# Attention and MLP on one core: another order of the same instructions on each engine

## The chip, the cores and the metric

The kernel runs on one core of a Trainium2 chip. The metric is device time in microseconds for one call, on the device's own clock. The engines of the core run side by side, each through its own queue in order: TensorE (matmuls; PE in the profile, its weight loads PEld), VectorE (DVE), ScalarE (ACT), and SyncE (SP), which here issues every transfer. An instruction that waits holds back all that stands behind it on its engine.

## The reference

Rotary attention over 4 batches, 8 heads, 576 positions, head size 64, and an MLP on its output (2304 rows, 512 to 2048 to 512).

```python
q_rot, k_rot = (rotate(q), rotate(k))
scores = scale * np.matmul(q_rot, k_rot.transpose(0, 1, 3, 2))
attn = np.exp(scores - np.max(scores, axis=-1, keepdims=True))
attn = attn / (np.sum(attn, axis=-1, keepdims=True) + 1e-09)
attn_out = np.matmul(attn, v)
# heads side by side: x is (2304, 512)
h = x @ w_in
g = np.where(h >= 1, h, np.where(h <= -1, 0.0, (h + 1) ** 2 / 4.0))
out = g @ w_out
```

## The kernel before

Every product is made of three half-precision matmuls: each float32 operand is split into a high part and the rest, in float16, and high·high, high·low and low·high are summed in PSUM. So K, Q, V, the attention weights, the attention output, the MLP's inner values and both weight matrices all pass through ACT (high part) and DVE (rest).

The work runs in eight blocks: for each batch a first one (row tiles 0 and 1 of 128 rows) and a last one (tiles 2 and 3, with the 64 rows left over). In a block, for each of four head pairs and each tile: `scores` (line 597; 12 matmuls into the two banks of `psS`; line 614 for the left rows), then the softmax on DVE and ACT (lines 570 to 582): negative maximum on DVE (L570), exponential with row sum on ACT (L572), reciprocal on DVE (L577), high part on ACT (L580) and rest on DVE (L582) into `phl`. A DMA transpose on SP (`dmaT`, L246) turns `phl` into `pT`. When the tiles of a head pair are there, 28 matmuls make the values (`values`, L632, into `psV`), and `x_out` (L643 ACT, L646 DVE) splits them into `xT`. The MLP of a block (`mlp_block`) runs after its attention: eight steps `m` of 2 × 12 matmuls (L711, into `psH`), an activation on ACT and DVE (L719 to L734) and 2 × 6 matmuls into `psO` (L743); at the end ACT brings `psO` out (L754) and SP stores it.

Beside the first blocks the weights are prepared: `prep_w` loads each of eight slices of `w_in` and `w_out` in two pieces (`dma`, L242), into buffers that are in use for something else before and after (other slices, `rv`, `kT`). DVE unpacks them (L518 to L522), ACT takes the high part (L531), and the rest comes from DVE (L540) or from TensorE and ACT (L549 to L553). `prep_v` splits V (ACT L462 high, DVE L466 rest; `vS`) and copies parts of it within SBUF (`vM`, three transfers). `prep_k` and `load_q` load K and Q of the next batch.

The order is written out by hand. Each piece of work enters a list with `plan.add` (engine, cost, what it reads and writes): 2,224 steps, 487 on TensorE, 751 on ACT, 777 on DVE, 209 on SP. `Plan.order` walks through the string `ORDER`: each number takes that element out of the steps still left. The steps are then emitted in that order, so each engine gets its own steps in it, and the waits follow from the data. The costs given to `plan.add`, with the transfer rates in `dma` (L242) and `dmaT` (L246), are not read when the kernel is built. Buffers are assigned when the steps are listed, not when they are emitted. A "place" below is a step's position in the order of its engine, counted from 0.

Of the kernel before, what the change touches and what calls it, by code (L numbers as in the profile page):

```python
# [24 lines left out]

ORDER = """
# [58 lines left out]
"""  # L85

PICK = set("""  # L90
lo0 lo12 lo15 m1.2 m1.6 m2.0 m2.1 m2.2 m2.3 m2.4 m2.7 m3.0 m3.1 m3.2 m3.3 m3.4 m3.5 m4.0 m4.1 m4.3 m5.2 m5.3
m5.4 m5.5 m6.0 m6.1 m6.2 m6.4 m6.5 m6.6 m6.7 m7.2 m7.4 m7.5 m8.2 m8.4 m8.5 m9.0 m9.1 m9.2 m9.3 v0 v1
""".split())
O_CHUNKS = 5


class Plan:
# [41 lines left out]
    def order(self, idle):  # L139
        left = list(range(len(self.steps)))  # L140
        return [partial(idle, *map(int, k[1:].split("."))) if k[0] == "*" else self.steps[left.pop(int(k))][3]
                for k in ORDER.split()]
# [3 lines left out]
def kernel(  # L146
# [12 lines left out]
    nc = tc.nc  # L159
    B, _, NP, S = km.shape[1:]  # L160
# [22 lines left out]
    vS = sbt("vS", [128, 2, T, H, D], F16)  # L183
# [734 lines left out]
```

## Time and profile before

| | us |
|---|---|
| median of 3 runs (613.07 to 615.18) | 614.44 |
| the profiled execution | 611.8 |
| its span, first to last instruction | 610.0 |
| PE / PEld busy | 569.6 / 367.9 |
| DVE / ACT busy | 483.2 / 457.7 |
| mean granted TensorE clock | 0.982 |

The first 100 us prepare operands while little of the attention runs; up to some 215 us attention, weights and the first MLP run together; from then on TensorE has a queue of MLP work. How to read the views: a row of the timeline names the start, the duration, the engine, the line, the operation, the tiles and their shapes; brackets at its end give how long the engine sat idle ahead of it and what ended the idle time. "PEclk" is the granted clock as a share of full speed (1.00 is 2.4 GHz, 0.50 is 1.2 GHz).

### The profile page before, as it was taken

What the parts mean: (1) busy time and instruction counts of PE and PEld (TensorE: products, weight loads), DVE (VectorE), ACT (ScalarE), POOL (GpSimd) and SP (SyncE); (2) the same over time, 40 slices, a digit from 0 to 9 for tenths busy, and PEclk for the clock granted to TensorE, in tenths of its full rate; (3) what the DMA queues carried; (4) which work ended last, traced back from release to release, by engine and by line L of the source; (5) the groups of instructions that cost most, each with busy time, mean ns of one, the idle gap of its engine ahead of it and who ended that gap; (6) DMA issues with size and microseconds to landing.
All of it is one profiled execution on the core that took longest, in us unless ns stands there. A gap on an engine that the chain in (4) does not pass through costs nothing.

```text
span 610.0 us, 12165 instructions
## 1 busy us (share of the span) xinstructions
PE 569.6 (93%) x4824; PEld 367.9 (60%) x4824; DVE 483.2 (79%) x782; ACT 457.7 (75%) x922; POOL 1.5 (0%) x11
## 2 busy tenths in 40 slices
PE   5677779999999969999999999999999999999996
PEld 3352435556666646666666766666666676667673
DVE  5998898999999959999889888987978757524341
ACT  4999787999999848788866788868876677553431
POOL 1000000000000000000000000000000000000000
PEclk9889898999999989999999999999999999999999
DMA  8889996685959978857599577575563836500000
GB/s 281 302 198 289 264 254 155 187 209 104 221 168 199 237 120 169 172 104 111 156 187 181 92 164 162 119 129 85 103 128 64 130 66 131 99 36 1 1 36 18
DMA packets 184009, 88.94 MB, mean 146 GB/s; under 512 B 170768, under 2 KB 172048, under 8 KB 183952
## 3 DMA queue, kind: packets, MB, share of 16 engines
q1 hardware_dynamic: 183952, 88.17, 65.5%
q8 instruction: 38, 0.62, 0.4%
q14 instruction: 19, 0.16, 0.1%
HBM read 38.60 MB, written 4.72 MB: 71 GB/s over the span
## 4 chain that ended last, share of the span: by engine, by line
PE 60%; DVE 8%; ACT 4%; DMA 3%; issue 1%; SPq 1%; ACTq 0%
PE psO L743 24%; PE psH L711 24%; PE psV L632 6%; PE psS L597 5%; DVE phl L582 2%; DMA pT<-phl 2%; DVE sca L570 2%; ACT p L572 1%; SPq L246 1%; DMA rv<-in_vm_dram 1%; DVE r L730 1%; PE psS L614 1%; ACT phl L580 1%; DVE g L734 1%; DMA vM<-vS 1%
## 5 line engine op out<-in xcount | busy, mean ns | idle before, releaser
L711 PE MATMUL psH<-xT,w 128*128 128x256 f16 (+1 forms) x1920 | 205.7, 262 | 0.6 <-ACT a L719 0.6
L743 PE MATMUL psO<-w,g 128*128 128x512 f16 x864 | 201.5, 379 | 0.0
L711 PEld LDWEIGHTS <-w 128*128 128x128 f16 x1920 | 170.7, 98 | 36.8 <-issue 5.0
L743 PEld LDWEIGHTS <-g 128*128 128x128 f16 x864 | 81.8, 98 | 84.6 <-DVE g L734 1.5
L572 ACT ACTIVATE p<-psS,sca 128x576 f32<-128x576 f32 x144 | 105.3, 734 | 26.3 <-DVE sca L570 18.1
L580 ACT ACTIVATE phl<-p,sca 128x576 f16<-128x576 f32 x144 | 108.2, 768 | 22.3 <-DVE sca L577 16.4
L582 DVE SCALAR_TENSOR_TENSOR phl<-p,sca,phl 128x576 f16<-128x576 f32 x144 | 115.9, 811 | 10.2 <-ACT phl L580 10.0
L570 DVE TENSOR_REDUCE sca<-psS 128x1 f32<-128x576 f32 x144 | 105.2, 750 | 14.3 <-PE psS L597 14.1
L734 DVE SCALAR_TENSOR_TENSOR g<-r,g 128x512 f16<-128x512 f32 x72 | 49.4, 686 | 32.5 <-ACT g L732 32.3
L597 PE MATMUL psS<-kT,qT 64*128 64x512 f16 (+1 forms) x768 | 61.3, 288 | 6.6 <-ACT p L572 6.4
L719 ACT ACTIVATE a<-psH 128x512 f32<-128x512 f32 x72 | 42.3, 587 | 33.0 <-PE psH L711 27.0
L730 DVE SCALAR_TENSOR_TENSOR r<-a,r 128x512 f32<-128x512 f32 x72 | 49.4, 687 | 20.1 <-ACT r L728 19.2
L732 ACT ACTIVATE g<-r 128x512 f16<-128x512 f32 x72 | 44.8, 623 | 26.4 <-DVE r L730 16.2
L597 PEld LDWEIGHTS <-qT 64*128 64x128 f16 x768 | 29.9, 95 | 50.0 <-issue 27.9
L632 PE MATMUL psV<-pT,vS 128*64 128x256 f16 (+1 forms) x512 | 44.3, 298 | 6.9 <-DMA pT<-phl 6.9
L632 PEld LDWEIGHTS <-vS 128*64 128x64 f16 x512 | 27.6, 114 | 14.3 <-DMA pT<-phl 7.3
L723 DVE SCALAR_TENSOR_TENSOR r<-a 128x512 f32<-128x512 f32 x38 | 26.1, 687 | 5.8 <-ACT a L719 4.5
L572 ACT ACTIVATION_READ_ACCUMULATOR p<-psS,sca 128x1 f32 x144 | 28.4, 197 | 0.0
L632 PE MATMUL psV<-pT,vM 128*64 128x256 f16 (+1 forms) x320 | 26.8, 300 | 0.1
L643 ACT ACTIVATE xT<-psV,sca 128x320 f16<-128x320 f32 (+1 forms) x24 | 13.7, 569 | 15.3 <-PE psV L632 15.3
L726 ACT ACTIVATE r<-a 128x512 f32<-128x512 f32 x34 | 21.3, 626 | 4.8 <-DVE g L734 4.5
L577 DVE RECIPROCAL sca<-sca 128x2 f32<-128x2 f32 x72 | 11.5, 160 | 15.9 <-ACT sca L575 15.3
(108 smaller groups left out, 486.4 us busy)
## 6 DMA issues: line engine op xcount, KB each, us to landing
w<-in_w_in_dram SPq DMA_DIRECT2D x14, 512.0 KB, 6.4
w<-in_w_out_dram SPq DMA_DIRECT2D x12, 512.0 KB, 7.9
rv<-in_vm_dram SPq DMA_DIRECT2D x8, 512.0 KB, 5.3
out_dram<-o SPq DMA_DIRECT2D x16, 256.0 KB, 2.5
rk<-in_km_dram SPq DMA_DIRECT2D x6, 576.0 KB, 5.7
dup<-in_km_dram SPq DMA_DIRECT2D x6, 576.0 KB, 4.5
rq<-in_qb_dram SPq DMA_DIRECT2D x4, 640.0 KB, 5.2
vM<-vS SPq DMA_DIRECT2D x8, 256.0 KB, 5.1
```

What stands on the lines that cost most here:

```text
L570: plan.add("dve", dve_cost(S, psum=True), at, lambda m=m, src=src: nc.vector.tensor_reduce(out=m, in_=src, op=ALU.max, axis=AX.X, negate=T ...
L572: plan.add("act", act_cost(S, psum=True, ptrs=2), at, lambda a=a, e=e, m=m, src=src: nc.scalar.activation(out=p32[e], in_=src, func=AF.Exp ...
L580: plan.add("act", act_cost(S), at, lambda a=a, e=e, hi=hi: nc.scalar.activation(out=hi, in_=p32[e], func=AF.Copy, scale=rr[:, a:a + 1]), r ...
L582: plan.add("dve", dve_cost(S, ptrs=1), at, lambda a=a, e=e, hi=hi, lo=lo: nc.vector.scalar_tensor_tensor(out=lo, in0=p32[e], scalar=rr[:, ...
L597: nc.tensor.matmul(out=psS[a][:, lo:hi], lhsT=qT[hf][d, l, j, c:c + 128], rhs=kT[ks][d, j, m, lo:hi], start=z == 0, stop=z == 2)
L632: nc.tensor.matmul(out=outs[a], lhsT=st, rhs=moving(a, blk), start=z == 0, stop=z == len(seq) - 1)
L711: nc.tensor.matmul(out=psH[:, n * i:n * i + n], lhsT=wi[ft // 2][:, wl, kk, 128 * (ft % 2):128 * (ft % 2) + 128], rhs=xfn(xl, kk), start=z ...
L719: plan.add("act", act_cost(512, psum=True, ptrs=0), at, lambda one=one: nc.scalar.activation(out=a, in_=psH, func=AF.Relu, scale=2.0 ** -7 ...
L730: plan.add("dve", dve_cost(512), at, lambda one=one: nc.vector.scalar_tensor_tensor(out=r, in0=a, scalar=one, in1=r, op0=ALU.max, op1=ALU. ...
L732: plan.add("act", act_cost(512, ptrs=0), at, lambda g=g, one=one: nc.scalar.activation(out=g[:, 0], in_=r, func=AF.Relu, scale=1.0, bias=- ...
L734: plan.add("dve", dve_cost(512), at, lambda g=g, one=one: nc.vector.scalar_tensor_tensor(out=g[:, 1], in0=r, scalar=-one, in1=g[:, 0], op0 ...
L743: nc.tensor.matmul(out=psO[pos[tt]], lhsT=g[:, gl, n * i + 128 * tt:n * i + 128 * tt + 128], rhs=wo[ft // 2][:, wl, ft % 2, :], start=ft = ...
```

## The change

`ORDER` is replaced by another list of the same length, found by a search over a cost model whose numbers were measured anew. In the plan the rate of an ordinary transfer goes from 400 to 329 bytes per ns, that of the copies within SBUF (`vM`) to 220, that of a transpose from 221 to 231 for 128 rows and to 195 for 64. The unused `idle` (extra matmuls for starred entries of the list) goes. No step is added or removed.

```diff
 ORDER = """
-5 4 1 2 28 1 0 3 51 1 76 27 0 23 47 3 3 25 95 118 95 116 95 46 129 129 157 226 146 71 21 3 0 8 2 20 0 41 16 18 3
+5 4 4 9 1 2 26 4 1 0 0 75 48 51 25 122 121 98 22 46 70 3 25 21 3 129 128 91 91 1 2 4 3 2 2 17 0 16 13 17 55 31
...
-2 3 3 3 3 0 0 0 0 0 0 0 0 0 1 0
+2 3 3 3 8 3 7 7 2 2 2 1 0 0 0 0 0 0 0 0 0 0 1 0
 """
...
-    def order(self, idle):
+    def order(self):
         left = list(range(len(self.steps)))
-        return [partial(idle, *map(int, k[1:].split("."))) if k[0] == "*" else self.steps[left.pop(int(k))][3]
-                for k in ORDER.split()]
+        return [self.steps[left.pop(int(k))][3] for k in ORDER.split()]
...
-    def dma(at, dst, src, r, w, nbytes, eng="sp", chain=[]):
+    def dma(at, dst, src, r, w, nbytes, eng="sp", chain=[], rate=329.0):
...
-        plan.add(eng, 480.0 if eng == "sp" else 1000.0, at, lambda: q.dma_start(out=dst, in_=src), r, w + chain, bw=nbytes / 400.0)
+        plan.add(eng, 480.0 if eng == "sp" else 1000.0, at, lambda: q.dma_start(out=dst, in_=src), r, w + chain, bw=nbytes / rate)
...
-        plan.add("sp", nbytes / 221.0 + 60.0, at,
-                 lambda: nc.sync.dma_start_transpose(out=dst, in_=src), r, w, bw=nbytes / 221.0, turn=True)
+        rate = 231.0 if src.shape[0] == 128 else 195.0
+        plan.add("sp", nbytes / rate + 60.0, at,
+                 lambda: nc.sync.dma_start_transpose(out=dst, in_=src), r, w, bw=nbytes / rate, turn=True)
...
-    def idle(b, n):
-        bank = (psH, psO[0], psO[1], psV, psS[0], psS[1])[b]
-        for _ in range(n):
-            nc.tensor.matmul(out=bank[:, 0:128], lhsT=idn, rhs=idn, start=True, stop=True)
-
-    order = plan.order(idle)
+    order = plan.order()
```

## Rows read from the trace of the kernel before

**Rows 1.** The page, first part: busy us, share, instructions of each engine.

```profile
PE 569.6 (93%) x4824; PEld 367.9 (60%) x4824; DVE 483.2 (79%) x782; ACT 457.7 (75%) x922; POOL 1.5 (0%) x11
```

**Rows 2.** Busy us of each engine by stretch; at the end clock, DMA share, GB/s.

```profile
0.00:58.00 58.00, 38.85 (x173) 23.08 (x173) 49.75 (x116) 47.72 (x107) 1.53 (x11) 0.91 0.88 267
58.00:98.00 40.00, 30.45 (x228) 16.13 (x227) 31.77 (x44) 29.61 (x59) 0.00 (x0) 0.91 1.07 255
98.00:213.00 115.00, 113.04 (x935) 70.95 (x937) 113.34 (x170) 110.20 (x217) 0.00 (x0) 1.00 0.79 182
...
230.00:605.40 375.40, 375.03 (x3364) 249.40 (x3362) 277.70 (x438) 260.37 (x521) 0.00 (x0) 1.00 0.54 107
```

**Rows 3.** The chain of waits in order of time: start, us, what.

```profile
213.98 5.76 DMA pT<-phl
...
502.68 2.73 PE psH L711 x24
505.40 3.88 PE psO L743 x18
```

**Rows 4.** Timeline of TensorE: three matmuls that follow idle time.

```profile
64.89 1.51 PE L549 MATMUL psO<-xT 128*128 128x512 f32 x2 [4.39 <-ACT w L553]
...
92.40 0.71 PE L632 MATMUL psV<-pT,vS 128*64 128x256 f16 x8 [2.08 <-DMA pT<-phl]
...
219.79 1.06 PE L632 MATMUL psV<-pT,vS 128*64 128x256 f16 x8 [4.78 <-DMA pT<-phl]
```

**Rows 5.** Timeline of DVE: three that follow idle time, and one split.

```profile
61.96 0.69 DVE L518 TENSOR_SCALAR o<-w 128x1024 uint32<-128x1024 uint32 x1 [3.71 <-DMA w<-in_w_out_dram]
...
82.52 0.81 DVE L582 SCALAR_TENSOR_TENSOR phl<-p,sca,phl 128x576 f16<-128x576 f32 x1
...
96.00 0.75 DVE L646 SCALAR_TENSOR_TENSOR xT<-psV,sca,xT 128x512 f16<-128x512 f32 x1 [2.56 <-ACT xT L643]
...
223.70 1.42 DVE L570 TENSOR_REDUCE sca<-psS 128x1 f32<-128x576 f32 x2 [6.10 <-PE psS L597]
```

**Rows 6.** Timeline of ACT: the second half of V, and a wait.

```profile
45.99 1.14 ACT L462 ACTIVATE vS<-rv,sca 128x1024 f16<-128x1024 f32 x1
...
63.49 0.78 ACT L580 ACTIVATE phl<-p,sca 128x576 f16<-128x576 f32 x1 [3.25 <-DVE sca L577]
```

**Rows 7.** Timeline of SP's DMA queue, 40 to 100 us.

```profile
41.77 4.31 SPq L246 DMA_TRANSPOSE pT<-phl  x1
...
51.25 1.16 SPq L242 DMA_DIRECT2D w<-in_w_out_dram  x2
...
81.46 8.94 SPq L246 DMA_TRANSPOSE pT<-phl  x2
```

**Rows 8.** Timeline of SP's DMA queue, 198 to 232 us.

```profile
198.74 8.91 SPq L246 DMA_TRANSPOSE pT<-phl  x2
207.70 0.58 SPq L242 DMA_DIRECT2D dup<-in_km_dram  x1
...
208.86 23.12 SPq L246 DMA_TRANSPOSE pT<-phl  x6
```

**Rows 9.** Tile `pT`, its transposes, 36:100 and 230:420: ns min/median/max.

```profile
L246 SPq DMA_TRANSPOSE pT<-phl x8: 3287/4142/9409, 36.0 to 91.6; - x8
...
L246 SPq DMA_TRANSPOSE pT<-phl x40: 1199/2666/5735, 229.5 to 419.3; - x40
```

**Rows 10.** By stretch, as rows 2: two with a lower clock.

```profile
66.00:69.00 3.00, 3.00 (x24) 1.88 (x24) 3.00 (x4) 3.00 (x9) 0.00 (x0) 0.51 1.05 266
...
219.70:223.00 3.30, 3.21 (x32) 2.45 (x34) 0.00 (x0) 0.13 (x1) 0.00 (x0) 0.57 0.77 144
```

**Rows 11.** DMA issues of the page: count, KB each, median us to landing.

```profile
w<-in_w_out_dram SPq DMA_DIRECT2D x12, 512.0 KB, 7.9
...
vM<-vS SPq DMA_DIRECT2D x8, 256.0 KB, 5.1
```

**Rows 12.** By stretch, as rows 2: the first 20 us of the full queue.

```profile
230.00:250.00 20.00, 20.00 (x188) 13.66 (x187) 19.19 (x32) 16.01 (x34) 0.00 (x0) 1.00 0.98 184
```

More of the change, by code (lines that the diff above doesn't have):

```diff
@@ L1 @@
 from contextlib import ExitStack
-from functools import partial
 import numpy as np
@@ L484, in prep_v @@
             r=["rvL", fk, ("vM", 0)], w=["vZ"])
-        dma(at, vM[0:64, 1:5], vS[64:128, 0], [("vS", 0, hf) for hf in range(2)], [("vM", 1)], 64 * 4096)
-        dma(at, vM[64:128, 0:4], vS[0:64, 0], [("vS", 0, hf) for hf in range(2)], [("vM", 2)], 64 * 4096)
-        dma(at, vM[64:128, 4], vM[0:64, 0], [("vM", 0)], [("vM", 3)], 64 * 1024)
+        dma(at, vM[0:64, 1:5], vS[64:128, 0], [("vS", 0, hf) for hf in range(2)], [("vM", 1)], 64 * 4096, rate=220.0)
+        dma(at, vM[64:128, 0:4], vS[0:64, 0], [("vS", 0, hf) for hf in range(2)], [("vM", 2)], 64 * 4096, rate=220.0)
+        dma(at, vM[64:128, 4], vM[0:64, 0], [("vM", 0)], [("vM", 3)], 64 * 1024, rate=220.0)
     vkeys = [("vS", l, hf) for l in range(2) for hf in range(2)] + [("vS", 1, hf, 0) for hf in range(2)] + [("vM", i) for i in range(4)] + ["vZ"]
```

112 rows, old and new, of the table ORDER are left out of this document.

## Prediction

> **What bounds the kernel now.** I read first the page's busy line [rows 1], then busy time by stretch [rows 2], then the chain of waits in order of time [rows 3], and from where the chain leaves TensorE the timelines of each engine [rows 4 to 8]. In [rows 2] see two regimes. From 230 to 605.4 us TensorE is busy 375.03 of 375.40 us, at full clock: nothing but its own queue matters there, and a reorder inside it gains nothing. Before, it idles: 58 − 38.85 = 19.2 us up to 58, 9.6 us from 58 to 98, 2.0 from 98 to 213. From 98 to 213 DVE is as full as TensorE (113.3 and 113.0 of 115). So every us of TensorE idle that goes before 230 comes off the end, provided DVE and ACT lose as much idle there.
>
> The Trainium skill ("Trainium Kernel Development and Optimization", Performance Expectations) says that matmul busy time misleads, since matmuls are pipelined, and that the weight loads' busy share is the better measure. By it TensorE would be 60% used [rows 1], and the reorder could also gain after 230 us, where weight loads fill 249 of 375 us. The trace decides otherwise: twenty-four 256-column matmuls take 2.73 us in the chain and eighteen of 512 take 3.88 us [rows 3], 114 and 216 ns apiece, 107 and 213 ns being the columns at 2.4 GHz. The array is full; I take no gain there.
>
> The idle that can go has three places outside the start:
> - A, 60.5 to 64.9: TensorE waits 4.39 us for ACT [rows 4], which waits 3.25 us for DVE [rows 6], which waits 3.71 us for a w_out load [rows 5]. The load was issued at 51.25 [rows 7] and used at 61.96. Then the clock is down: granted 0.51 from 66 to 69, the 1.2 GHz level, TensorE busy all of it [rows 10]: 3.0 × 0.49 = 1.5 us.
> - B, 90 to 96: TensorE waits 2.08 us for a transpose [rows 4], DVE then 2.56 us [rows 5].
> - C, 215 to 219.8: TensorE waits 4.78 us for a transpose [rows 4], DVE 6.10 us for scores queued behind that on TensorE [rows 5]. The clock again: 0.57 for 3.3 us [rows 10], 3.2 × 0.43 = 1.4 us.
>
> **The change part by part.** No instruction is added or taken away. The rates in the helpers feed only the plan's costs, which nothing reads when the list is followed; the removed `idle` was not used, since the list has no starred entry. Both cost nothing. What is left is the order. I laid both lists against the plan's 2,224 steps: 156 of 487 TensorE steps leave their place (by at most 8), 338 of 751 on ACT, 391 of 777 on DVE, 98 of 209 on SP. For each step I added the work ahead of it on its engine, at the time from its start to the next start in the traced run, in the old and the new order; "ahead +x" is the difference.
>
> A. On SP the two w_out pieces of slice 2 stood at places 32 and 39 and now stand at 33 and 31, ahead of the transpose of head pair 1 (place 30, now 34; issued at 41.77 for 4.31 us [rows 7]). Loads that nobody needs yet move behind: w_out of slice 6 into `rv` from 36 and 48 to 56 and 55, w_in of slice 7 into `kT` from 41 to 61; both pieces of slice 3 and the vM copies pass behind too. The pieces should leave by the 46.1 at which that transpose ended. With the old 10.7 us from issue to use they land at 56.8, with the 7.9 us median of w_out loads [rows 11] at 54. DVE reaches the instruction at 61.96 − 3.71 = 58.25 and has +0.1 us ahead. So DVE's 3.7 us go; TensorE's 4.4 and the clock's 1.5 can go only as far as DVE and ACT follow. Gain between 3.7 and 5.9; I take 4.5, nearer the DVE row, since DVE sets the pace there. What is late next: two vM copies now wait at the head of SP (places 39 and 38) for ACT's second half of V [rows 6], +7.9 us ahead: 47.1 + 7.9 = 55.0. Landing 5.1 us later [rows 11], at 60.1, against TensorE's first values step at 66.8 − 4.4 = 62.4. The cover is 2.3 us; if the copies take the 10.7 us of the load above, it costs 3.3 us.
>
> B. Four transposes now follow each other (places 45 to 48; before 46, 49, 53, 54), with loads of slices 4 to 6 behind. The fourth went out at the end of the pair issued at 81.46 and 8.94 us long [rows 7]. DVE wrote the last of its data by 83.3 [rows 5] and has −1.7 us ahead of that now, so it should go at about 81.6 minus what A brings, and take 3.3 us, the shortest of that stretch [rows 9], and be through by 85. The values step then waits for nothing. Gain: 2.1 (TensorE) to 2.6 (DVE), plus up to another 1.5 of clock; I take 2.5. Behind these transposes now wait the second w_out piece of slice 4 and w_in of slice 5: they leave at about 85 less A's gain, where the old ones left at 80; DVE comes to the first of them at 87 less that gain, with +4.4 us ahead, so 6 us of cover stand against the 7.9 of a median load, and up to 1.9 us are owed if nothing else yields.
>
> C. On TensorE four steps, 4.8 us of work (three of the MLP at 1.3 us [rows 3] and a scores step), move ahead of the last two values steps of the block. On SP the K load at 207.70 and the Q load behind it, which ran before the transposes from 208.86 [rows 8], change place: K's from 102 to 92, Q's from 103 to 110. DVE's 6.10 us go with it, as the scores step now stands before the values. What is late next is the row of transposes itself: the first of it must wait for an earlier values step, which let it go at 198.74 [rows 8] and is also 4.8 us later, so it starts at 203.5. Four of them at 2.67 us (median from 230 to 420 [rows 9]) end at 214.2, at 5 us at 223.5; TensorE wants the last at 219.8, where the old one landed. With most loads gone from between them I take some 3.3 us each, 216.7, no wait. Gain 4.8 to 6.2, taken 5.5; with 5 us each 3.7 less.
>
> The start (0 to 58) is crowded by ACT and DVE (47.7 and 49.8 of 58 busy [rows 2]). At 58 both have the same work ahead (ACT +0.2, DVE +0.1). DVE fills early idle with K and Q products; ACT's first exponentials come 0.7 us sooner in its queue, while the maxima they wait for have +1.7 us ahead on DVE, so ACT idles up to 2.3 us there. From −2 (gain) to +2: I take 0.
>
> The rest (98 to 213, and after 230): TensorE has no idle to lose, so an order can only cost. Of some 325 steps after 230, ten are now ahead of the ACT step they need by more than their old slack, by 1.4 to 2.7 us, in three clusters (253 to 310, 490 to 510, 584); ACT and DVE can run ahead in most of it. Between 0 and 7.1 us (the largest of each cluster: 2.3 + 2.7 + 2.1); I take 2.5.
>
> Sum: 4.5 + 2.5 + 5.5 − 2.5 = 10.0 us. The profiled execution took 611.8 us, of it 610.0 the span; the median of the runs is 614.44, 2.6 us more, spread 2.1. The difference has nothing to do with the order, so I take 10.0 off the median: 604.4.
>
> **The rivals.**
> 1. One of the gains is lost. Either the transposes of C still take 5 us each (C then gives 5.5 − 3.7 = 1.8), or TensorE, ACT and DVE hand to each other so often from 58 to 98 that DVE's idle moves instead of going (A and B give 2). For it: eight transposes before 100 us took up to 9.4 us, median 4.1 [rows 9], with the transfers full. Against: fewer loads between them now. Gain about 5: 609.
> 2. It does not do what it says: each wait gone returns nearby, the DVE-full stretch from 98 to 213 [rows 2] gives all back. Against: DVE is idle in A, B and C too. 614.
> 3. Slower: TensorE runs in order, and the scores steps of 253 to 310 are pulled up 2 to 2.6 us while the exponentials that free their bank are not. There DVE has no room (19.19 of 20 us busy [rows 12]). If no stall relieves the next, the ten waits of that kind sum to 20 us: 614.4 − 12.5 + 20 = 622. It decides once TensorE idles over 12.5 us after 230; today it is 0.4.
>
> **How the numbers follow.** Forecast 604.4 with chance 0.63; rival 1 (609) 0.20; rival 2 (614) 0.09; rival 3 (622) 0.08. The forecast's own range: all gains at their upper ends and no new wait, 5.9 + 4.1 + 6.2 = 16.2, gives 598.2; lower ends and 2.5 of new waits, 3.7 + 2.1 + 4.8 − 2.5 = 8.1, gives 606.3. The range reaches over rival 1 into the edge of rival 2: 598.2 to 613.0. Faster by over 0.3% (about what a measurement of this kernel can tell from no change), below 612.6: forecast and rival 1, 0.83. Within 0.3%: 0.09. Slower: 0.08.
>
> **What the changed profile would show.** A right: DVE's instruction on that w_out piece follows its predecessor with under 1 us idle, and no half clock near 66. B right: the values step near 90 starts without a wait on `pT`. C right: no wait on `pT` on TensorE over 1 us after 200, and the granted clock 1.00 from then on. The stretch from 58 to 98 would hold over 34 us of TensorE work instead of 30.45. Wrong if TensorE shows new waits on ACT after 230, if the first values step waits for vM, or if the transposes still take 5 us.

## The result and the profile after

The changed kernel takes 598.82 us (median of 4 runs, 598.44 to 600.27) against 613.76 us of the kernel before, run beside it (4 runs, 612.28 to 615.18): a ratio of 0.9761, 95% interval 0.9731 to 0.9791. The forecast was 604.4, the range 598.2 to 613.0: faster, as predicted, 5.6 us below the forecast and 0.6 us above the lower end of the range. The profiled execution took 598.4 us, 596.7 of it the span. Before it was 611.8 and 610.0, so the traces show 13.4 us of the medians' 14.9.

Busy time by stretch, answering [rows 2] (PE, PEld, DVE, ACT, POOL; clock, DMA share, GB/s):

```profile
0.00:58.00 58.00, 37.29 (x170) 21.16 (x171) 50.44 (x117) 47.81 (x108) 1.54 (x11) 0.94 0.94 274
58.00:98.00 40.00, 37.24 (x289) 21.66 (x290) 39.02 (x53) 37.08 (x73) 0.00 (x0) 0.96 1.07 242
98.00:213.00 115.00, 111.83 (x970) 71.14 (x968) 111.10 (x170) 106.63 (x214) 0.00 (x0) 1.00 0.83 182
213.00:230.00 17.00, 17.00 (x160) 11.23 (x157) 16.52 (x28) 15.41 (x34) 0.00 (x0) 1.00 0.91 183
230.00:592.00 362.00, 361.42 (x3243) 239.93 (x3241) 265.23 (x418) 248.23 (x497) 0.00 (x0) 1.00 0.53 108
```

See two changes. From 58 to 98 TensorE works 37.24 us instead of 30.45, and DVE and ACT rise with it by 7 us each. From 213 to 230 TensorE has no idle left. After 230 it idles 0.6 us, so no new waits.

TensorE's timeline: the first values step, the fourth, and the last two of the block, answering [rows 4]:

```profile
62.52 0.63 PE L630 MATMUL psV<-pT,vS 128*64 128x256 f16 x8
...
84.70 0.60 PE L630 MATMUL psV<-pT,vS 128*64 128x256 f16 x8
...
210.56 0.63 PE L630 MATMUL psV<-pT,vS 128*64 128x256 f16 x8
...
212.37 0.63 PE L630 MATMUL psV<-pT,vS 128*64 128x256 f16 x8
```

None has the bracket of a wait; before, there was 2.08 us ahead of the fourth and 4.78 ahead of the last. DVE's timeline, answering [rows 5]: the w_out piece of A behind its predecessor, the second w_out piece of slice 4 that B pushes back, and an MLP product that matters for C:

```profile
56.49 1.21 DVE L520 SCALAR_TENSOR_TENSOR xT<-w,xT 128x1024 uint32<-128x1024 uint32 x1
57.63 0.68 DVE L516 TENSOR_SCALAR o<-w 128x1024 uint32<-128x1024 uint32 x1
...
85.12 0.69 DVE L516 TENSOR_SCALAR o<-w 128x1024 uint32<-128x1024 uint32 x1
...
204.16 0.69 DVE L732 SCALAR_TENSOR_TENSOR g<-r,g 128x512 f16<-128x512 f32 x1
```

SP's queue, answering [rows 7, 8] (start, time to the end of the last of the group, count). These are the times that SP spends on a transfer; its data land later:

```profile
65.38 14.68 SPq L244 DMA_TRANSPOSE pT<-phl  x4
80.11 0.57 SPq L239 DMA_DIRECT2D w<-in_w_out_dram  x1
...
195.85 5.61 SPq L244 DMA_TRANSPOSE pT<-phl  x2
201.51 0.58 SPq L239 DMA_DIRECT2D rv<-in_vm_dram  x1
202.20 8.69 SPq L244 DMA_TRANSPOSE pT<-phl  x2
```

The chain of waits at C shows how close it was:

```profile
206.84 0.74 DVE phl L580
...
207.63 4.69 DMA pT<-phl
...
212.37 1.72 PE psV L630 x28
```

SP was done with the last transpose of the row at 210.89, but its data landed at 212.32, 0.05 us before TensorE's step. The time without work ahead of that step is 0.09 us, too short for a bracket. B was as close: the w_out piece that left at 80.11 landed 4.9 us later, at 85.00, and DVE used it at 85.12.

The clock, answering [rows 10], with one stretch that is new:

```profile
66.00:69.00 3.00, 2.98 (x42) 2.02 (x40) 3.00 (x6) 2.97 (x8) 0.00 (x0) 1.00 1.01 358
78.00:82.00 4.00, 3.97 (x8) 2.02 (x9) 4.00 (x6) 3.72 (x7) 0.00 (x0) 0.57 1.02 188
210.00:214.00 4.00, 3.91 (x68) 3.17 (x64) 3.33 (x6) 3.42 (x7) 0.00 (x0) 1.00 0.64 140
```

Both half-clock stretches of [rows 10] are gone, and so is the one at B (92 to 96: 0.60 before, 1.00 after); a new one stands at 78 to 82, behind a wait of TensorE for ACT:

```profile
76.31 0.37 PE L612 MATMUL psS<-kT,qT 64*64 64x512 f16 x1 [1.40 <-ACT p L570]
```

Where the 13.4 us arise, read off single TensorE steps in both traces: the scores step of 58.33 starts at 58.99 (0.7 later), the first values step at 62.52 instead of 66.76 (4.2 sooner), the first MLP step at 89.90 instead of 97.93 (8.0), the MLP step of 209.74 at 202.05 (7.7), the values step of 284.92 at 271.65 (13.3), and it is 13.3 at the end. So by these two traces A gave 4.9 us, B 3.8, C 5.6, and nothing is given back after 230.

### The profile page after: what moved, and what is told of

Read it like the earlier page. It is cut to its first block, busy times and chain, and to the rows that moved or that the text cites. A ratio compares the mean times of both kernels' runs of the same rounds, so it can differ in the third digit from the quotient of the medians.

```text
span 596.7 us, 12159 instructions
## 1 busy us (share of the span) xinstructions
PE 564.8 (95%) x4824; PEld 365.1 (61%) x4824; DVE 482.3 (81%) x782; ACT 455.9 (76%) x922; POOL 1.5 (0%) x11
## 4 chain that ended last, share of the span: by engine, by line
PE 64%; DVE 15%; ACT 10%; DMA 7%; issue 3%; SPq 1%; DVEq 0%; ACTq 0%
PE psO L741 25%; PE psH L709 24%; PE psV L630 7%; PE psS L595 5%; DMA pT<-phl 3%; DVE phl L580 3%; DVE sca L568 3%; ACT p L570 2%; ACT phl L578 2%; DMA w<-in_w_out_dram 2%; DVE g L732 1%; PE psO L547 1%; DVE r L728 1%; DMA w<-in_w_in_dram 1%; DMA rk<-in_km_dram 1%
## 5 line engine op out<-in xcount | busy, mean ns | idle before, releaser
L595 PE MATMUL psS<-kT,qT 64*128 64x512 f16 (+1 forms) x768 | 59.7, 284 | 2.9 <-ACT p L570 2.7
L630 PE MATMUL psV<-pT,vS 128*64 128x256 f16 (+1 forms) x512 | 42.4, 288 | 1.7 <-DMA pT<-phl 1.7
L630 PE MATMUL psV<-pT,vM 128*64 128x256 f16 (+1 forms) x320 | 25.0, 286 | 0.0
L726 ACT ACTIVATE r<-r 128x512 f32<-128x512 f32 x34 | 21.3, 627 | 0.6
L644 DVE SCALAR_TENSOR_TENSOR xT<-psV,sca,xT 128x320 f16<-128x320 f32 (+1 forms) x24 | 14.6, 610 | 7.7 <-ACT xT L641 7.7
```

The source lines that it names most:

```text
L595: nc.tensor.matmul(out=psS[a][:, lo:hi], lhsT=qT[hf][d, l, j, c:c + 128], rhs=kT[ks][d, j, m, lo:hi], start=z == 0, stop=z == 2)
L630: nc.tensor.matmul(out=outs[a], lhsT=st, rhs=moving(a, blk), start=z == 0, stop=z == len(seq) - 1)
```

## The experiments

The theory from the prediction: three places on SP and TensorE make the gain, and they add. Seven kernels make some of those moves, and nothing else, in the kernel before; three undo one of them in the kernel after; two join one kernel's order to the other's. In the diffs a row is a stretch of one engine's order: T is a transpose with its head pair (2 and 3 for the first row tile, 12 and 13 the same pairs for the second), w_in and w_out carry their slice, K, Q, V are loads. The starts of six TensorE steps in every trace (us):

| | first values | fourth values | first MLP | last values of the block | values, 285 | last matmul |
|---|---|---|---|---|---|---|
| before | 66.76 | 92.40 | 97.93 | 219.79 | 284.92 | 605.0 |
| a_wout | 63.65 | 90.24 | 95.77 | 219.12 | 284.98 | 605.4 |
| b_turns | 65.39 | 97.37 | 102.61 | 226.22 | 291.74 | 611.3 |
| ab_sp | 64.34 | 98.16 | 103.55 | 226.65 | 292.55 | 613.2 |
| abc | 63.68 | 99.27 | 105.38 | 230.73 | 294.67 | 614.5 |
| ab_w41 | 63.68 | 90.41 | 94.31 | 220.19 | 285.53 | 606.0 |
| c_pe | 65.84 | 91.91 | 98.23 | 224.03 | 287.85 | 608.5 |
| c_sp | 65.79 | 91.72 | 98.06 | 218.77 | 284.15 | 603.9 |
| h_new_old | 63.42 | 85.78 | 90.98 | 215.21 | 280.99 | 601.7 |
| h_old_new | 65.69 | 92.14 | 98.44 | 220.53 | 279.95 | 600.7 |
| after_no_a | 63.21 | 90.41 | 96.22 | 218.73 | 278.18 | 598.4 |
| after_no_b | 63.10 | 95.04 | 101.96 | 223.35 | 282.66 | 603.3 |
| after_no_c | 62.66 | 85.00 | 90.20 | 213.40 | 283.56 | 603.6 |
| after | 62.52 | 84.70 | 89.90 | 212.37 | 271.65 | 591.7 |

Kernels whose TensorE order is that of before are compared with before, those with that of after with after. One profile stands for one execution: b_turns, c_pe, c_sp and h_old_new have before's order on every engine up to 66 us, and start the first values step 0.9 to 1.4 us sooner than it did. So differences of 1 us in the table say nothing, and verdicts rest on the medians.

**a_wout**, A's two w_out pieces alone (the loads of slices 6 and 7, which the prediction's A moves behind as well, stay):

```diff
-T 1, vM, w_out 2, vM, w_in 3, K, w_out 6, w_in 3, vM, w_out 2
+w_out 2, w_out 2, T 1, vM, vM, w_in 3, K, w_out 6, w_in 3, vM
```

> The order of before with two entries moved on SP alone: both w_out pieces of slice 2 stand ahead of the transpose of head pair 1. Theory (the gain of 58 to 65 us is the place of this load on SP): DVE's 3.7 us wait on w<-in_w_out near 62 us and TensorE's 4.4 us wait on w behind it go, the first MLP step (97.9 us before) starts 3.7 to 5.9 us sooner, and the end follows: 608 to 610 us by the median of before. Rival (the three engines hand to each other so often there that idle moves instead of going, and it takes the new compute order of the change to use the earlier load): the wait on w_out goes, but the first MLP step starts less than 2 us sooner, 612 to 614 us.

Measured: 612.90 us against 614.54, ratio 0.998 (0.996 to 1.0001): 1.6 us less, not clear of noise. DVE's wait is gone:

```profile
57.87 1.21 DVE L519 SCALAR_TENSOR_TENSOR xT<-w,xT 128x1024 uint32<-128x1024 uint32 x1
59.00 0.69 DVE L515 TENSOR_SCALAR o<-w 128x1024 uint32<-128x1024 uint32 x1
```

TensorE needs 4.5 us from the scores step (59.17) to the first values step, 8.4 in the profile of before: 3.9 us gained. But the four kernels with before's order there need only 6.4 to 6.8; DVE's wait is 2.48 to 2.67 us in three of them (2.30 in b_turns, where TensorE ends it), where [rows 5] have 3.71, and the clock from 66 to 69 is at 1.00, where [rows 10] have 0.51. In c_pe:

```profile
61.63 0.69 DVE L515 TENSOR_SCALAR o<-w 128x1024 uint32<-128x1024 uint32 x1 [2.67 <-DMA w<-in_w_out_dram]
```

So the one profile showed A at its dearest, and alone it brings some 2 us. A new wait stands right behind:

```profile
68.40 0.63 PE L629 MATMUL psV<-pT,vS 128*64 128x256 f16 x8 [1.95 <-DMA pT<-phl]
```

The second values step starts no sooner than in the four kernels with before's order (68.13 to 68.57), as it waits for a transpose that went out at 53.75, behind the loads left in front of it, and held SP for 11.09 us. In the kernel after, which has the loads of slices 6 and 7 further back, the same transpose takes 4.41 us (at 56.75), and nothing waits for it.

The 2 us stand at the first MLP step all the same (2.2), and at 285 us none is left. They went on SP. The pair of transposes behind two loads started 2.0 us sooner, but took 9.22 us, 7.82 in the kernel before, and the row behind it ended only 0.7 us sooner:

```profile
186.53 9.22 SPq L243 DMA_TRANSPOSE pT<-phl  x2
```

```profile
188.56 7.82 SPq L246 DMA_TRANSPOSE pT<-phl  x2
```

```profile
219.12 1.06 PE L629 MATMUL psV<-pT,vS 128*64 128x256 f16 x8 [4.91 <-DMA pT<-phl]
```

TensorE waits 4.91 us at C, as before. DVE's wait goes where it stands, and the transposes ahead of C and at C take the gain back.

**b_turns**, B alone:

```diff
-T 2, w_out 4, w_out 6, T 12, w_in 5, w_in 5, w_out 4, T 3, T 13
+w_out 4, T 2, T 12, T 3, T 13, w_out 6, w_in 5, w_in 5, w_out 4
```

> The order of before with SP alone changed between 80 and 100 us: the four transposes of head pairs 2, 12, 3 and 13 stand in one row, the loads that stood between them (w_out and w_in of slices 4 to 6) behind them. Theory: the waits of 2.1 us (TensorE) and 2.6 us (DVE) on pT near 92 to 96 us go, the four transposes take some 3.5 us each instead of 4.5 to 5, the first MLP step starts 2.1 to 4.1 us sooner; 610.3 to 612.3 us by the median of before, less if the loads behind them are then late. Rival: the last transpose is held by DVE's writing of its data and not by the loads, or the loads pushed behind are late by as much; under 1 us sooner, 613 to 615 us.

Measured: 620.60 us, ratio 1.0101 (1.0069 to 1.0133): slower. DVE and SP:

```profile
83.48 0.74 DVE L567 TENSOR_REDUCE sca<-psS 128x1 f32<-128x576 f32 x1
93.45 0.69 DVE L515 TENSOR_SCALAR o<-w 128x1024 uint32<-128x1024 uint32 x1 [9.22 <-DMA w<-in_w_out_dram]
```

```profile
67.45 16.42 SPq L243 DMA_TRANSPOSE pT<-phl  x4
83.92 0.57 SPq L239 DMA_DIRECT2D rv<-in_w_out_dram  x1
...
85.50 10.87 SPq L239 DMA_DIRECT2D w<-in_w_out_dram  x2
```

The row of four works as a row, its transposes taking 5.77, 2.70, 2.71 and 2.75 us, with 2.3 us between the third and the fourth in which SP waited for DVE's write of pair 13. But the w_out piece behind it left at 85.50 and landed 7.9 us later. DVE wanted it at 84.2 and stood 9.22 us, and ACT and TensorE behind it. It was the cover of the piece pushed back that broke. Half of it is the piece's place: it is the last of four loads here and the first in the kernel after, and the first of the four here left at 83.92 and landed at 88.72, 4.6 us ahead of it.

**ab_w41**, A, and B with that one piece ahead of the row:

```diff
-T 2, w_out 4, w_out 6, T 12, w_in 5, w_in 5, w_out 4, T 3, T 13
+w_out 4, w_out 4, T 2, T 12, T 3, T 13, w_out 6, w_in 5, w_in 5
```

> The order of before with SP alone changed: both w_out pieces of slice 2 ahead of the transpose of head pair 1, and the four transposes in one row as in ab_sp, but with the second w_out piece of slice 4 ahead of the row instead of behind it; the loads into rv and of slice 5 stay behind. Theory (the row cost time because that one piece was then late: DVE waited 9 us on it): the wait goes, the first MLP step (97.9 us before) starts 2 to 5 us sooner than in the kernel before, some 8 to 10 us sooner than in ab_sp, and what is left at the end is 610 to 614 us. Rival (the row itself is slow, as SP waits at its head for DVE's write of the last pair): the step starts no sooner than in a_wout less 2 us, the end at 614 us or more.

Measured: 611.26 us against 614.07, ratio 0.9952 (0.9931 to 0.9973). The first MLP step starts at 94.31, 3.6 us sooner than before and 9.2 sooner than in ab_sp (103.55), with no wait of DVE at that piece:

```profile
87.20 0.68 DVE L515 TENSOR_SCALAR o<-w 128x1024 uint32<-128x1024 uint32 x1
```

So the 9 us of b_turns were the one late load. Of the 3.6 us a wait of 1.72 us for ACT at 105.76 takes back a half, and the transposes ahead of C and at C the rest, as in a_wout: this execution has none of it left at 285 us. The medians keep 2.8 us.

**ab_sp** (the diffs of a_wout and b_turns together) and **abc** (these and the diff of c_pe, below):

> The order of before with the two SP edits (w_out pieces of slice 2 ahead of the transpose of head pair 1; four transposes in one row) and nothing else. Theory (they add): the first MLP step starts 7 to 9 us sooner, 605 to 607 us by the median of before. Rival (one takes what the other would have gained, as both release the same row of steps from 60 to 96 us): no more than the larger of the two alone, some 4 us, 610 us.

> The three edits together in the order of before: the two w_out pieces ahead of the transpose of head pair 1 and the four transposes in one row on SP, and the four steps ahead of the last two values steps on TensorE. Seven or so entries moved out of 2,224. Theory (these are the change, and they add): A and B bring 7 to 9 us at the first MLP step, C 5 to 6 us near 220, the end at 599 to 602 us, within 3 us of the changed kernel. Rival (the gain needs the many moved compute steps): 604 us or more.

Measured: 623.29 us, ratio 1.0137 (1.0099 to 1.0174), and 621.57 us, 1.0150 (1.0099 to 1.0200). For ab_sp theory and rival both expected a gain; the rival of abc (604 us or more) holds, but named no loss. The loss has the reason of b_turns: DVE stands 9.50 and 9.12 us for the w_out piece behind the row, and the first MLP step starts at 103.55 and 105.38. So these moves by themselves cost 7 to 9 us. They are not all that the prediction named: SP's part of C (c_sp, below) and the loads that A moves behind are in neither kernel, and no run has all of them together.

**c_pe**, TensorE's part of C alone (MLP m is its step m of that block):

```diff
-values, values, scores, MLP 7, MLP 5, MLP 5, MLP 7
+MLP 5, MLP 7, MLP 7, scores, values, values, MLP 5
```

> The order of before with TensorE alone changed at one place: three MLP steps and a scores step (4.8 us of work) move ahead of the last two values steps of the block (215 to 220 us). Theory: TensorE's 4.8 us wait on pT near 219.8 us and DVE's 6.1 us wait on scores go, no half clock follows: 4.8 to 6.2 us less at the end, 607.5 to 609 us by the median of before, and nothing before 200 us differs. Rival (the transposes are the bound there, and only moving the K and Q loads on SP brings them forward): less than 2 us, 612 to 614 us.

Measured: 614.19 us, ratio 1.0004 (0.9989 to 1.0019): the same. The wait on `pT` is gone, and others stand in its place:

```profile
218.04 1.04 PE L740 MATMUL psO<-w,g 128*128 128x512 f16 x4 [2.24 <-DVE g L731]
...
222.47 0.63 PE L629 MATMUL psV<-pT,vS 128*64 128x256 f16 x8
...
230.41 1.59 PE L594 MATMUL psS<-kT,qT 64*128 64x512 f16 x11 [2.15 <-ACT p L569]
```

```profile
217.31 0.68 DVE L731 SCALAR_TENSOR_TENSOR g<-r,g 128x512 f16<-128x512 f32 x1
```

The MLP product that TensorE now wants at 215.8 is made by DVE at 217.3. In the kernel after DVE makes it at 204.16 and is done 0.9 us ahead of TensorE (205.71). Pulling work into a wait needs its operands made earlier on the other engines too: C is not an order of TensorE alone.

**c_sp**, SP's part of C alone:

```diff
-T, T, K, Q, T, T
+T, T, T, T, K, Q
```

> The order of before with SP alone changed near 208 us: one K load and one Q load that stood ahead of the last two transposes of the block stand behind them. Theory (loads among the transposes both hold SP and lengthen the transposes): the last two start 1.2 us sooner and take 3 us each instead of 5.0 and 3.8, TensorE's 4.8 us wait on pT shrinks to 1 us or less, 610 to 611 us at the end. Rival (the wait is made by TensorE's and DVE's order, not by the loads): the wait stays over 3 us, 613 to 615 us.

Measured: 609.75 us, ratio 0.9923 (0.9897 to 0.9949), 4.3 us less by the medians (1.1 us by the two profiled executions, of which before's was 2.3 us below this median):

```profile
199.92 15.61 SPq L243 DMA_TRANSPOSE pT<-phl  x4
215.58 0.58 SPq L239 DMA_DIRECT2D dup<-in_km_dram  x1
```

```profile
218.77 0.63 PE L629 MATMUL psV<-pT,vS 128*64 128x256 f16 x8 [2.27 <-DMA pT<-phl]
```

The last two transposes took 2.40 and 3.52 us instead of 5.03 and 3.78, and TensorE's wait fell from 4.78 to 2.27 us. The wait left lies between theory and rival: the first two of the row, still behind three loads, took 5.39 and 3.95. Two entries on SP bring what TensorE's reorder alone doesn't.

**after_no_a, after_no_b, after_no_c**: one move of the kernel after undone.

```diff
 SP, after_no_a
-w_out 2, w_in 2, w_out 2, T 1, w_in 3, w_in 3, w_out 3, vM, vM, T 11
+w_in 2, T 1, w_in 3, w_in 3, w_out 3, vM, vM, w_out 2, w_out 2, T 11
 SP, after_no_b (and one w_out 6 to behind the first w_in 3)
-w_out 4, T 2, T 12, T 3, T 13, w_out 4, w_in 5, w_in 5
+T 2, w_out 4, w_out 6, T 12, w_in 5, w_in 5, w_out 4, T 3, T 13
 TensorE, after_no_c
-MLP 4, MLP 5, MLP 7, MLP 7, scores, values, values, scores
+values, values, MLP 4, MLP 5, MLP 7, MLP 7, scores, scores
```

> The order of after with the two w_out pieces of slice 2 moved back on SP to where they stood before, behind the transpose of head pair 1 and the vM copies. Theory: DVE waits on w<-in_w_out again near 62 us, 3.7 to 5.9 us come back by the first MLP step and stay to the end, 602.5 to 604.7 us by the median of after. Rival (after's compute order hides the later load): under 2 us, 599 to 601 us.

> The order of after with the loads of slices 4 to 6 put back between the four transposes on SP. Theory: the wait on pT near 85 us returns, 2.1 to 4.1 us come back by the first MLP step, 601 to 603 us by the median of after. Rival (the transposes are led by DVE's data, and the loads between them cost nothing): under 1 us, 598.5 to 600 us.

> The order of after with the last two values steps of the block put back on TensorE right behind the MLP step that they followed before, the K and Q loads on SP left where after has them. Theory (TensorE's order makes the gain near 220 us): TensorE waits on pT again for 3 to 5 us near 205 to 212 us and the end is 4 to 6 us later, 603 to 605 us by the median of after. Rival (the loads moved off the transposes on SP make it): under 2 us later, 599 to 601 us.

Measured, beside 614.03 us of before: 605.35 us (ratio 0.9853, 0.9825 to 0.9882), 609.73 us (0.9928, 0.9901 to 0.9955) and 610.99 us (0.9948, 0.9928 to 0.9969). Against the 598.82 of after that is 6.5, 10.9 and 12.2 us lost: together 29.6, twice the whole gain. Two of them undo more than their move. In after_no_a both w_out pieces stand behind two vM copies and three loads of slice 3; before has the first of them ahead of all these, and the second ahead of one. In after_no_c the values steps follow the scores of the left rows, as in before, but a step of MLP 4 stands behind them that before has ahead. The waits that came back, in after_no_a, after_no_b, and on two engines in after_no_c:

```profile
65.11 0.69 DVE L513 TENSOR_SCALAR o<-w 128x1024 uint32<-128x1024 uint32 x1 [6.71 <-DMA w<-in_w_out_dram]
```

```profile
95.04 1.06 PE L627 MATMUL psV<-pT,vS 128*64 128x256 f16 x8 [6.11 <-DMA pT<-phl]
```

```profile
210.46 1.07 PE L627 MATMUL psV<-pT,vS 128*64 128x256 f16 x8 [5.94 <-DVE xT L641]
```

```profile
222.15 1.42 DVE L565 TENSOR_REDUCE sca<-psS 128x1 f32<-128x576 f32 x2 [10.73 <-PE psS L592]
```

Each place was named rightly, but the price is above the forecast, as the other engines' orders count on the move: DVE comes to the w_out load at 58.4, when its first piece has only just been issued (57.40). In the order of before the second piece left at 51.25; here SP stood from 51.8 to 56.2 at the vM copies, for ACT's second half of V, which after makes later. The transposes of after_no_b end at 93.0 instead of 80.1. In after_no_c it isn't `pT` that TensorE waits for, as the theory said: it waits for DVE to take the preceding values out of `psV`, which after's DVE order does as late as 210.4, and DVE then starves 10.73 us for scores.

**h_new_old and h_old_new**, the two halves on every engine, joined at the first MLP step:

```diff
 each engine, h_new_old
-the order of before up to the first MLP step
+the order of after up to the first MLP step
 each engine, h_old_new
-the order of before from the first MLP step on
+the order of after from the first MLP step on
```

> On every engine the order of after up to the first MLP step (near 90 us), then all that is left in the order of before. Theory (the gain of 58 to 98 us is carried to the end): first MLP step 7 to 8.5 us sooner than before, the waits near 220 us as before, end 605 to 608 us. Rival (the row of transposes near 200 to 220 us takes it back, as it took the 2 us of a_wout): the lead at the first MLP step is there but by 285 us it is under 3 us, 611 to 614 us.

> On every engine the order of before up to the first MLP step (near 98 us), then all that is left in the order of after. Theory (the gain near 220 us comes from the orders after 98 us alone): the first MLP step starts as before, no wait on pT over 1 us near 220 us, 4.8 to 7 us sooner from there on, end 607 to 609 us. Rival (the order of after near 200 us needs the lead that it brought along): under 2 us, 612 to 614 us or more.

Measured, beside 614.07: 607.76 us (ratio 0.9902, 0.9874 to 0.9930) and 607.20 us (0.9889, 0.9872 to 0.9907): 6.3 and 6.9 us less, together 13.2 of the 14.9. TensorE at the last values step, in the one and the other:

```profile
215.21 1.07 PE L627 MATMUL psV<-pT,vS 128*64 128x256 f16 x8 [5.76 <-DMA pT<-phl]
```

```profile
220.53 0.63 PE L627 MATMUL psV<-pT,vS 128*64 128x256 f16 x8
```

The first half alone leads by 7.0 us at the first MLP step and keeps 3.9 by 285 us: 1.4 us go before C (5.6 are left at the third values step of that block), and C costs it 1.6 us more than it costs before (a wait of 5.76 us, then the clock at 0.81 from 213 to 230, before 0.90). The second half alone has no lead to bring along and needs none: no wait at C. The halves are separate gains, and add nearly. Of the single moves within them only c_sp keeps a gain of that size (4.3 us).

## Why the prediction came out

By its own steps:
- A, taken 4.5 (3.7 to 5.9), gave 4.9 by the two profiles. The signs named for it all show: DVE without idle, no half clock near 66, 37.24 us of TensorE work from 58 to 98. The vM copies landed at 60.7, where 60.1 was expected, and TensorE wanted them at 62.5: the cover held. The size was luck in part. Against c_pe, c_sp and h_old_new, which keep before's order up to 98 us, it is 3.2: from the scores step to the first values step they need 6.7 us (the mean), after 3.5. The step that was mis-sized is the price of one stall, taken from one execution in which DVE came to the load 0.7 us sooner, and the load 0.3 to 0.5 us later, than in the others.
- B, taken 2.5 (2.1 to 4.1), gave 3.8 by the two profiles, and 5.1 against the same three kernels (32.5 us from the first values step to the first MLP step, after 27.4), where A is smaller. The term was too small: it left out a wait of TensorE for ACT ahead of the scores step at 89.42 (1.20 us; 2.24 to 2.83 in those three), and took next to nothing for the clock, which was at 0.60 from 92 to 96 and in those three at 0.50 to 0.52 from 92 to 97. A and B together gave 8.3 to 8.7, taken 7.0. Named as owed if nothing else yields: up to 1.9 us for the w_out piece behind the row. Nothing was owed, by a hair: the row began early enough for the piece to leave at 80.11, and as the first load behind the row it landed 4.9 us later, where the median of 7.9 was taken; with 7.9 DVE would have stood 2.9 us. b_turns shows that debt at 9.2 us where nothing yields and the piece is the last of four, with DVE at the piece 1.3 us before it was even issued. The prediction's 6 us of cover were 5.0 in the full order, and hold for it alone.
- C, taken 5.5 (4.8 to 6.2), gave 5.6. The row's start, 203.5 less the lead of 7.7, was put at 195.8, and it was 195.85. Its four transposes took SP 2.80, 2.71, 3.97 and 3.26 us, where 3.3 each was taken. But the working set SP's end (216.7) against the time at which the old transpose had landed (219.8), and left out that the data land later: 2.0 us later before (SP's end 217.76, landed 219.75), 1.4 us here. And it left out that SP stands 1.5 us ahead of the fourth, for DVE's write of its data (206.84 in the chain above). So of the 3 us of cover 0.05 was left; that there is no wait is luck.
- The start, taken 0: 0.7 us later than in the profile of before at the step of 58.33, but the four kernels with before's order there, named above, are 0.6 to 0.8 us later too. So it is 0.
- New waits after 230, taken −2.5: none. This is the step that failed. It compared each step's shift with the slack in the old trace, as if ACT and DVE entered 230 us in their old state. But from 213 to 230 DVE now works 16.52 us and ACT 15.41 of 17, before 10.66 and 9.11: the exponentials that TensorE's pulled-up scores steps need were no longer late. That these 6 us are what covers them is argued from the two traces, not tried.

The sum by the traces: 4.9 + 3.8 + 5.6 − 0.7 less 0.3 lost from 98 to 213 is 13.3. Without the term for new waits the forecast would have been 601.9; A and B together, 1.7 us above what was taken, make it 600.2. The rest lies between traces and medians: before's profiled execution ran 2.6 us below its first median, after's 0.4 below. One reason may be the half clock at C, which is not the same in each execution: from 213 to 230 the granted clock was 0.90 in the profile of before, and 0.80 in that of a_wout, whose wait there is as long. That is argued only.

What the prediction did not say, and the runs show, is that its moves are not the gain by themselves. Made alone, A's gave 1.6 us, which is not clear of noise, B's cost 6, TensorE's part of C gave nothing and SP's part 4.3; A and B together cost 9, with TensorE's part of C 7. The place of each stall and what ended it were read rightly. The traces suggest that the price is collected only when the steps around it move too, DVE's use of the pushed-back load and its earlier MLP product above all; no run tries these one by one. Rival 2 (each wait gone returns) comes nearest to what happened to A: in a_wout and h_new_old some of a lead goes again, but to the transposes some 100 us later, where that rival had DVE take it. In the full order the lead stays. Not tried either: the order of after on one engine with that of before on the others, which would tell how much of the gain each engine's order carries.

The counts of moved steps (156, 338, 391 and 98) are the fewest that have to be moved to turn one order into the other. By place, as that word is used here, 352, 633, 672 and 175 steps differ.

No kernel run here beats the changed one. The 1.40 us wait at 76.31 and the half clock behind it are still open there (4 us at 0.57, some 1.7 us); that was not tried.

## What to carry to other kernels

A stall's price in a trace is what removing it can bring, and not what the one move that removes it brings: for each thing pushed back, find the engine that uses it next and when, and for each step pulled forward, who makes its operand. Undoing one move in the new order shows where it sits, not what it is worth: here the three undone cost 29.6 us of a 14.9 us gain. Try the move alone in the old order too. And set the time at which a transfer lands, not the time at which its queue is done with it, against the time at which it is wanted.

## What the runs showed of the hardware

A transpose on SP's queue takes longer behind a load than behind another transpose. In the 14 traces, from 60 to 230 us, the 88 transposes of 128 rows issued within 0.3 us behind a load held SP for 2.73 to 7.15 us, median 4.94; the 77 issued so behind another of 128 rows held it for 2.40 to 4.01, median 2.82 (28 behind one of 64 rows: median 3.39). Their data landed 7.8 and 4.8 us after the start, in the median. The four of after's row from 65.38 took 6.07, 2.85, 2.71 and 2.75. So a load between two transposes costs its own 0.5 us on SP and some 2.1 us on the transpose behind it, and a row of transposes pays this once, at its first. c_sp shows it by a move: with two loads taken out from ahead of them, two transposes went from 5.03 and 3.78 to 2.40 and 3.52 us. The Trainium skill ("DMA: Bandwidth & Descriptors", Queues, rings and completion order) says that what one engine issues goes through one ring on each of the same 16 engines and is consumed there in ring order; by that a transpose would stand behind the rest of a load, and these rows agree.

The clock fell after short waits of TensorE as well: behind the 1.40 us at 76.31 it was at 0.57, near the 1.2 GHz level, for 4 us; in c_sp, behind 2.27 us, eight matmuls of one kind went from 0.63 us to 1.07. The wait alone does not decide it: behind waits of 2.97 to 3.35 us near 64 us, in b_turns, c_pe, c_sp and h_old_new, the clock was at 1.00 from 66 to 69.
